# Two accumulator tiles in place of one, and a new timetable for the gated products after attention

## The chip, the cores and the metric

One core of a Trainium2 chip runs the whole program. Its engines each take their own instructions in order: TensorE (PE; its weight loads are shown as PEld), VectorE (DVE), ScalarE (ACT), GpSimd (POOL) and SyncE (SP), which issues nearly all DMAs. An engine whose next instruction has to wait for a semaphore holds everything behind it. The metric is the device time of one execution in microseconds.

## The reference, cut to what matters

```
q, k, v: (4, 8, 576, 64)             w_in: (512, 1024)  conv_w: (3, 1024)  w_out: (1024, 512)
q_rot, k_rot = rotate(q), rotate(k)                    # rotary tables
scores = q_rot @ k_rot^T / 8;  attn = softmax(scores)  # over 576 keys
x = (attn @ v), heads side by side                     # (4, 576, 512)
h = max(x @ w_in, 0)                                   # (4, 576, 1024)
conv_out = sum over k of conv_w[k] * h shifted by k-1  # three taps along the sequence
out = (h * sigmoid(conv_out)) @ w_out                  # (4, 576, 512)
```

The weights arrive as 64-bit floats and are turned into fp32 in the kernel.

## The kernel before, in words

**Pairs and steps.** Two heads of one batch make a pair: 16 pairs. The 576 queries of a pair are cut into four blocks of 128 and one of 64 for both heads, so a pair has five *steps*, s = 0 to 4, and the whole attention has 80, numbered n = 5p + s. A table `plan[n]` holds, for every step n, closures with a rank; they are run in the order of their ranks, and that order is the order of instructions on every engine (nothing is reordered afterwards).

**What a step holds.** PE makes the scores of step n (`emit_S`, L260, "S", tile `sp`); DVE takes two row maxima (L268, `negm`); ACT takes two exponentials (L272, `st`). PE turns the exponentials of step n-1 around (`emit_T`, L320, "the turn", tile `tp`) and ACT copies them into `pt` (L198). The last 64 keys of one head and the first of the other are turned by two small transposes (`emit_Trem`, L357, "the remainder's turn"), which write columns 320 to 383 of both accumulator banks and are copied to `pt` by DVE (L200). In the step after a pair's last one, n = 5p + 5, PE multiplies `pt` by v (`emit_E`, L388, two products of 20 matmuls, "E"); ACT copies each (L398, `xn`), DVE scales it some steps later (L402) by 1/sum, which reaches it by way of two DMAs (`rd`, `rb`), and ACT and POOL split it into a high and a low fp32r part (`xT`, L406, L407).

**The two products of the second stage.** From step 26 (`WIDE`) on the weights are ready, and steps also hold *units* of the first product (`emit_M1`, L421: 12 matmuls, 128 of the 1024 columns for 288 tokens) and *halves* of the second (`m2_half`, L519: 48 matmuls of 64 rows, 256 of the 512 output columns for 128 tokens). Behind a unit come, on other engines: ACT's max (L429, `rr`), three DVE taps ("the taps", L433 once, L435 twice, tile `c`), ACT's tanh (L441), DVE's gate (L444), ACT's high part (L452, `g`) and POOL's low part (L453). A half ends in an ACT copy (L533) of one bank, a DVE add (L534) of the other and a store. `UNITS` and `HALVES` say which step holds how many; `E` of step 5p + 5 ranks last.

**The timetable of what follows a unit.** `defer(k, fn)` puts a closure k *slots* ahead; a slot passes (`tick`) after each closure whose rank is in `onpe`, so after each piece of PE work. The taps, tanh, gate and split come 2, 5, 7 and 9 slots after the unit, wherever these slots fall.

**The accumulator.** `m_pair` takes, once a step, one tile `pm` of two banks (128 x 2 x 512 fp32) from a pool with one buffer, so the next step's tile is the same two banks. Units, halves, E and the remainder's turn of a step all live in it; `m_tile` hands out the two banks in turn.

**Other work of a pair.** Its q and k are loaded (L148 to L150, six DMAs each), rotated on POOL ("the rope", L189 six times, L192 three times) and turned on DVE (L233, L236, L242), 9 to 2 steps before the pair begins.

**The tail.** After the last step the pools are closed and the units and tiles that are left run back to back in six other banks (`mt`, L421 and L499): 16 units, and the tiles of the second product from the second half of tile 10 to tile 17.

Of the kernel before, what the change touches and what calls it, by code (L numbers as in the profile page):

```python
# [7 lines left out]
F32 = mybir.dt.float32  # L8
# [12 lines left out]
def attention_moe_kernel(ctx, tc, q, k, v, w_in, conv_w, w_out, tab, tabx, out):  # L21
# [49 lines left out]
    sinr = tabs[:, 576:640].rearrange("p (n i) -> p n i", n=2)  # L71
    ptctx = ExitStack()
    ptp = ptctx.enter_context(tc.tile_pool(name="ptp", bufs=1, side="right"))
    late = {"tail": False, "short": False, "u": 0}
    pt = ptp.tile([128, 9, S], F32, name="pt")

    slot = [0]
# [28 lines left out]

    def m_pair():
        if pair["n"] != late["n"]:
            pair.update(n=late["n"], ps=psum["m"].tile([128, 2, 512], F32, tag="m", name="pm"), k=0)
        return pair["ps"]  # L110

    def m_tile():
        if late["tail"]:
            return psum["t"].tile([128, 512], F32, tag="mt", name="mt")
        ps = m_pair()
        pair["k"] ^= 1
        return ps[:, 1 - pair["k"], :]

    raw = {}
    rot = {}  # L120
# [225 lines left out]
    def emit_Trem(p, s):  # L346
        x = ST[p, s].rearrange("p h k -> p (h k)")[:, 512:640]
        dst = pt[:, 8, 128 * s:128 * s + 128]
        if "m" not in psum:
            ps = spare(128)  # L350
            nc.tensor.transpose(ps, x, idf)
            after(lambda: evac("V", dst, ps))
            return
        ps = m_pair()[:, :, 320:384]
        for r in range(2):
            i = slice(64 * r, 64 * r + 64)
            nc.tensor.transpose(ps[:, r, :], x[i], idf[i, i])  # L357
        at(late["n"], 5, lambda: evac("V", dst.rearrange("p (r c) -> p r c", r=2), ps))

    rb = {}  # L360

# [46 lines left out]

        norms[p, j] = lambda: (norm(), defer(1, split))

    def emit_M1(blk, f):
        b, j = divmod(blk, 2)
        g, rr = late["g"], late["rr"]
        ps = m_tile()
        fs = slice(128 * f, 128 * f + 128)
        n = 3 * NK
        i = 0
        for kk in range(NK):
            xs = xslot[b, kk, j]
            for w, e in ((winh, 0), (winh, 1), (winl, 0)):  # L420
                nc.tensor.matmul(  # L421
                    out=ps[:, 0:XW], lhsT=w[:, kk, fs], rhs=xT[:, xs, e, :], start=(i == 0), stop=(i == n - 1)
                )
                i += 1
        if f == NF - 1:
            for kk in range(NK):
                free_slots.append(xslot.pop((b, kk, j)))
        r = rr[(blk * NF + f) % len(rr)]
        nc.scalar.activation(out=r[:, 1:XW], in_=ps[:, j:j + XW - 1], func=AF.Relu, scale=0.5)  # L429
        c = late["pc"].tile([128, HS], F32, tag="c", name="c")  # L430

        def conv():
            nc.vector.tensor_scalar(out=c, in0=r[:, j:j + HS], scalar1=cw[:, f:f + 1], scalar2=None, op0=ALU.mult)  # L433
            for e in (1, 2):
                nc.vector.scalar_tensor_tensor(  # L435
                    out=c, in0=r[:, j + e:j + e + HS], scalar=cw[:, 8 * e + f:8 * e + f + 1], in1=c,
                    op0=ALU.mult, op1=ALU.add,
                )

        def tanh():  # L440
            nc.scalar.activation(out=c, in_=c, func=AF.Tanh)  # L441

        def gate():
            nc.vector.scalar_tensor_tensor(  # L444
                out=c, in0=c, scalar=1.0, in1=r[:, j + 1:j + 1 + HS], op0=ALU.add, op1=ALU.mult
            )

        def split():
            o = 0
            for dst, n in g_pieces(blk, f):  # L450
                hi, lo = dst[:, 0, :], dst[:, 1, :]
                nc.scalar.activation(out=hi, in_=c[:, o:o + n], func=AF.Copy)  # L452
                nc.gpsimd.tensor_tensor(out=lo, in0=c[:, o:o + n], in1=hi.bitcast(F32), op=ALU.subtract)  # L453
                o += n
            ready.add((blk, f))

        lag = (1, 2, 3, 4) if late["short"] else (2, 5, 7, 9)
        for k, fn in zip(lag, (conv, tanh, gate, split)):
            defer(k, fn)

    LASTB = 2 * B - 1
    TAIL = (LASTB * HS + 127) // 128 * 128
# [24 lines left out]
    done_tt = set()  # L487

    def emit_M2(tt, part):
        cuts = 2 if tt in (len(HALVES) // 2, B * S // 128 - 1) else 1  # L490
        per, width = cuts * NF // 4, DM // cuts
        cut, part = divmod(part, 4 // cuts)
        cols = slice(width * cut, width * cut + width)
        if part == 0:
            ops[tt] = m_tile()
        for f in range(per * part, per * part + per):
            assert all((blk, f) in ready for blk in range(tt * 128 // HS, (tt * 128 + 127) // HS + 1))
            for i, (e, w) in enumerate(((0, wouth), (0, woutl), (1, wouth))):
                nc.tensor.matmul(  # L499
                    out=ops[tt][:, 0:width], lhsT=g_tile(tt, f, e), rhs=w[:, f, cols],  # L500
                    start=(f == 0 and i == 0), stop=(f == NF - 1 and i == 2),
                )
        if part == 4 // cuts - 1:
            done_tt.add(tt)
            ot = late["po"].tile([128, DM], F32, tag="ot", name="ot")[:, 0:width]
            nc.vector.tensor_copy(ot, ops.pop(tt)[:, 0:width])
            nc.sync.dma_start(out=out[tt * 128:tt * 128 + 128, cols], in_=ot)

    def m2_half(tt, cut):
        cols = slice(256 * cut, 256 * cut + 256)  # L510

        def run(fs):
            ps = m_pair()
            for f in fs:
                assert all((blk, f) in ready for blk in range(tt * 128 // HS, (tt * 128 + 127) // HS + 1))
                for i, (e, w) in enumerate(((0, wouth), (0, woutl), (1, wouth))):
                    for r in range(2):
                        rows = slice(64 * r, 64 * r + 64)
                        nc.tensor.matmul(  # L519
                            out=ps[:, r, 0:256], lhsT=g_tile(tt, f, e)[rows], rhs=w[rows, f, cols],  # L520
                            start=(f == 0 and i == 0), stop=(f == NF - 1 and i == 2),
                        )

# [3 lines left out]
        def second():  # L527
            run(range(NF // 2, NF))
            if cut:
                done_tt.add(tt)  # L530
            ps = m_pair()
            ot = late["po"].tile([128, 256], F32, tag="oh", name="oh", bufs=2)
            nc.scalar.activation(out=ot, in_=ps[:, 0, 0:256], func=AF.Copy)  # L533
            nc.vector.tensor_tensor(out=ot, in0=ot, in1=ps[:, 1, 0:256], op=ALU.add)  # L534
            nc.sync.dma_start(out=out[tt * 128:tt * 128 + 128, cols], in_=ot)

        return first, second
# [102 lines left out]
        wsteps += wcv[i][1:]  # L640

    WIDE = 26
    UNITS = dict([(n, 1) for n in (26, 27, 28, 29, 31, 32, 33, 34)])
    UNITS.update({36: 3, 38: 3, 41: 2, 44: 2, 47: 3, 49: 3, 53: 3, 56: 3, 58: 2, 64: 2, 67: 3, 69: 3, 73: 3, 76: 3, 78: 2})
    HALVES = [37, 39, 42, 43, 46, 48, 51, 52, 54, 57, 59, 61, 62, 63, 66, 68, 71, 72, 74, 77, 79]
    plan = {}
    onpe = (0, 0.5, 1, 2, 3, 4, 10)
    engines = {nc.tensor.engine, nc.vector.engine, nc.scalar.engine, nc.gpsimd.engine, nc.sync.engine}

    def at(n, rank, fn):  # L650
# [2 lines left out]
    def emit():  # L653
        with tc.manual_schedule(engines=engines):
# [17 lines left out]
            for p in range(1, NP):  # L672
                n = STEPS * p
                for i, part in enumerate("qk"):
                    if p > 1:
                        at(n - 9 + 2 * i, 19, lambda p=p, part=part: load(p, part))
                    at(max(n - 6 + i, 0) if p > 1 else 0, 18, lambda p=p, part=part: rope(p, part))
                    at(max(n - 4 + 2 * i, 2), 0.45, lambda p=p, part=part: emit_TQ(p, part))
                at(n + 3, 19, lambda p=p: load_v(p))
            for p in range(NP):  # L680
                n = STEPS * p
# [29 lines left out]
            at(12, 3, conv_cw)  # L711
            at(14, 2, turn_cw)
            for n, k in UNITS.items():
                for _ in range(k):
                    blk, f = divmod(late["u"], NF)
                    late["u"] += 1
                    at(n, 2, lambda blk=blk, f=f: emit_M1(blk, f))
            for i, n in enumerate(HALVES):
                for k, u in enumerate(m2_half(i // 2, i % 2)):
                    at(n, 2 + k, u)  # L720
            for n in range(max(plan) + 1):
                late["n"] = n
                late["short"] = n >= STEPS * NP - 3
                if n == WIDE:
                    wctx.close()
                    ectx.close()
                    psum_pools(actx, s=2, t=2, m=1)
                    gpool = ctx.enter_context(tc.tile_pool(name="gpool", bufs=1))
                    late["pc"] = ctx.enter_context(tc.tile_pool(name="pc", bufs=4))
                    late["po"] = ctx.enter_context(tc.tile_pool(name="po", bufs=1))  # L730
# [5 lines left out]
                while plan.get(n):  # L736
                    e = min(plan[n], key=lambda e: e[:2])
                    plan[n].remove(e)
                    e[2]()
                    if e[0] in onpe:  # L740
                        tick()
            while due:
                tick()
# [8 lines left out]
            first = [lambda f=f: emit_M1(last, f) for f in range(NF)]  # L752
            second = [lambda f=f: emit_M1(LASTB, f) for f in range(NF)]
            t = HS * last // 128
            prev = m2_units(len(HALVES) // 2, t)[len(HALVES) % 2 * 2:]
            seq = prev[:len(prev) - NF]
            for a, b in zip(first, prev[len(prev) - NF:]):
                seq += [a, b]
            for u in seq + second + m2_units(t, B * S // 128):
# [54 lines left out]
```

## Time and profile before

| | |
|---|---|
| time, median of 3 runs | 555.95 us (555.48 to 556.79) |
| the profiled execution's own time | 555.18 us |
| its span, first to last instruction | 553.4 us, mean granted TensorE clock 0.988 |
| PE busy | 466.4 us (84%), 4692 instructions |
| PEld busy | 363.6 us (66%) |
| DVE busy | 355.9 us (64%), 689 |
| ACT busy | 314.8 us (57%), 842 |
| POOL busy | 297.1 us (54%), 479 |
| chain that ended last | PE 44%, DVE 24%, ACT 21%, issue 4%, DMA 3% |

Busy time is the union of an engine's instructions over the whole span; the chain is followed back from the last instruction, each time to what released it. Both are averages over four stages that differ: attention with the conversion of the weights (to 128.3 us), steps 26 to 35, steps 36 to 79, and the tail from 482.1 us. The steps can be found in the trace by their scores: each run of eight L260 matmuls opens one.

### The profile page before, as it was taken

The numbers are of one execution on the slowest core, as the hardware profiler recorded it, in microseconds if no ns is written. First come the engines' busy times: TensorE is split into PE (matmuls) and PEld (weight loads), VectorE is DVE, ScalarE is ACT, GpSimd is POOL, SyncE is SP. The second block draws the span as 40 slices with busy tenths as digits, with TensorE's granted clock in tenths as the row PEclk, the third lists the DMA queues.
The fourth block names the chain that finished last, engine by engine and source line by source line (L and its number), as shares of the span: only waits on it lengthen the run. The fifth ranks groups of instructions, "written<-read, shape, count | busy, mean of one in ns | idle before, by whom it ended". The sixth has DMA issues, their size and how long they took to land.

```text
span 553.4 us, 12460 instructions
## 1 busy us (share of the span) xinstructions
PE 466.4 (84%) x4692; PEld 363.6 (66%) x4692; DVE 355.9 (64%) x689; ACT 314.8 (57%) x842; POOL 297.1 (54%) x479
## 2 busy tenths in 40 slices
PE   2877777868899878898888978998879887899997
PEld 1344545535676766767667776786758766699986
DVE  4798889983878565645675666446765626256941
ACT  2678777874866556646565555656548536334510
POOL 3799979998478373372475236445293013123430
PEclk9999999988999999999999998999999998999999
DMA  9787675553332331233306023252222001001011
GB/s 213 161 164 178 160 187 144 125 108 77 55 81 51 65 74 32 55 75 75 75 23 127 34 48 70 62 108 51 45 55 63 12 23 33 32 9 39 2 38 58
DMA packets 140849, 42.73 MB, mean 77 GB/s; under 512 B 132189, under 2 KB 135797, under 8 KB 140789
## 3 DMA queue, kind: packets, MB, share of 16 engines
q1 hardware_dynamic: 139444, 41.54, 33.7%
q8 instruction: 37, 0.61, 0.4%
q10 hardware_dynamic: 1344, 0.39, 0.3%
q14 instruction: 24, 0.19, 0.1%
HBM read 37.12 MB, written 4.79 MB: 76 GB/s over the span
## 4 chain that ended last, share of the span: by engine, by line
PE 44%; DVE 24%; ACT 21%; issue 4%; DMA 3%; POOL 2%; SPq 1%; ACTq 0%; DVEq 0%; POOLq 0%
PE pm L421 9%; ACT st L272 8%; DVE negm L268 8%; PE pm L388 8%; PE mt L499 8%; PE sp L260 6%; ACT pt L198 6%; PE pm L519 5%; PE mt L421 5%; DVE c L435 4%; ACT rr L429 3%; PE tp L320 1%; DVE c L444 1%; DVE c L433 1%; DVE wt L557 1%
## 5 line engine op out<-in xcount | busy, mean ns | idle before, releaser
L268 DVE TENSOR_REDUCE negm<-sp 128x1 f32<-128x576 f32 x144 | 102.2, 746 | 42.0 <-PE sp L260 35.7
L453 POOL TENSOR_TENSOR g<-c,g 128x288 fp32r<-128x288 f32 (+4 forms) x88 | 53.5, 623 | 133.3 <-ACT g L452 133.1
L272 ACT ACTIVATE st<-sp,negm 128x576 f32<-128x576 f32 x128 | 93.8, 739 | 53.8 <-DVE negm L268 53.3
L421 PE MATMUL pm<-xT,winh 128*128 128x290 f32 x384 | 85.9, 316 | 25.7 <-ACT rr L429 25.7
L260 PE MATMUL sp<-kT,qT 64*128 64x288 f32 (+4 forms) x556 | 97.9, 460 | 3.8 <-DVE kT L236 2.6
L198 ACT ACTIVATE pt<-tp 128x512 f32<-128x512 f32 (+3 forms) x176 | 84.0, 529 | 6.5 <-PE tp L320 6.1
L421 PEld LDWEIGHTS pm<-xT,winh 128*128 128x128 f32 x384 | 62.4, 194 | 33.1 <-ACT rr L429 31.6
L435 DVE SCALAR_TENSOR_TENSOR c<-rr,cw,c 128x288 f32<-128x288 f32 x128 | 77.0, 602 | 4.5
L407 POOL TENSOR_TENSOR xT<-xn,xT 128x290 fp32r<-128x290 f32 x32 | 27.4, 869 | 75.5 <-ACT xT L406 75.5
L320 PEld LDWEIGHTS tp<-idf,st 64*128 64x128 f32 x1024 | 43.1, 139 | 33.2 <-ACT st L272 22.7
L519 PE MATMUL pm<-wouth,g 64*128 64x256 f32 x672 | 64.3, 281 | 0.0
L320 PE MATMUL tp<-idf,st 64*128 64x64 f32 x1024 | 50.5, 228 | 16.1 <-ACT st L272 15.6
L260 PEld LDWEIGHTS sp<-kT,qT 64*128 64x128 f32 (+1 forms) x556 | 47.4, 177 | 23.8 <-issue 9.9
L189 POOL TENSOR_TENSOR rk<-rk,tabt 128x192 f32<-128x192 f32 x90 | 57.1, 669 | 10.8 <-DVE c L435 7.3
L388 PE MATMUL pm<-pt,vm 128*64 128x290 f32 x368 | 50.0, 413 | 13.3 <-ACT xn L398 8.2
L189 POOL TENSOR_TENSOR rq<-rq,tabt 128x192 f32<-128x192 f32 x90 | 56.4, 661 | 6.9 <-DMA rq<-q 6.6
L421 PE MATMUL pm<-xT,winl 128*128 128x290 f32 x192 | 57.8, 301 | 0.0
L519 PEld LDWEIGHTS pm<-wouth,g 64*128 64x128 f32 x672 | 56.2, 186 | 0.0
L519 PE MATMUL pm<-woutl,g 64*128 64x256 f32 x336 | 50.4, 276 | 0.0
L429 ACT ACTIVATE rr<-pm 128x289 f32<-128x289 f32 x48 | 20.1, 419 | 49.3 <-PE pm L421 49.3
L200 DVE COPY pt<-pm 128x128 f32<-128x128 f32 x44 | 12.6, 287 | 54.3 <-ACT rr L429 54.2
L388 PEld LDWEIGHTS pm<-pt,vm 128*64 128x64 f32 x368 | 25.4, 136 | 33.2 <-ACT xn L398 13.9
(108 smaller groups left out, 865.0 us busy)
## 6 DMA issues: line engine op xcount, KB each, us to landing
rq<-q SPq DMA_DIRECT2D x30, 144.0 KB
rq<-q SPq DMA_DIRECT2D x60, 72.0 KB
rk<-k SPq DMA_DIRECT2D x30, 144.0 KB
rk<-k SPq DMA_DIRECT2D x60, 72.0 KB
w<-moe_w_in SPq DMA_DIRECT2D x8, 512.0 KB
vm<-v SPq DMA_DIRECT2D x32, 128.0 KB
w<-moe_w_out SPq DMA_DIRECT2D x8, 512.0 KB
out<-oh SPq DMA_DIRECT2D x21, 128.0 KB
```

Of the source, the lines that this page charges most:

```text
L189: nc.gpsimd.tensor_tensor(out=y, in0=y, in1=tabt[:, a:a + 3], op=ALU.mult)
L198: nc.scalar.activation(out=out, in_=in_, func=AF.Copy, scale=1.0 if sc is None else sc)
L260: nc.tensor.matmul(out=out, lhsT=qt[64 * h:64 * h + 64, c], rhs=kt[64 * h:64 * h + 64, a:a + n], start=True, stop=True)
L268: reds.setdefault((p, s), []).append(lambda: nc.vector.tensor_reduce(out=nm, in_=sc, axis=AX.XY if len(sc.shape) == 3 else AX.X, op=ALU.ma ...
L272: lambda: nc.scalar.activation(out=dst, in_=sc, func=AF.Exp, bias=nm, scale=1.0, accum_out=sm)
L320: nc.tensor.transpose(ps[r][:, 64 * k:64 * k + 64], x[i], idf[i, i])
L388: nc.tensor.matmul(out=xp[64 * h:64 * h + 64, :], lhsT=vmain[p][:, h, i, :] if i < 4 else vrem[:, h, :], rhs=pt[:, 2 * i + h if i < 4 else ...
L421: nc.tensor.matmul(out=ps[:, 0:XW], lhsT=w[:, kk, fs], rhs=xT[:, xs, e, :], start=(i == 0), stop=(i == n - 1))
L435: nc.vector.scalar_tensor_tensor(out=c, in0=r[:, j + e:j + e + HS], scalar=cw[:, 8 * e + f:8 * e + f + 1], in1=c, op0=ALU.mult, op1=ALU.add,)
L453: nc.gpsimd.tensor_tensor(out=lo, in0=c[:, o:o + n], in1=hi.bitcast(F32), op=ALU.subtract)
L499: nc.tensor.matmul(out=ops[tt][:, 0:width], lhsT=g_tile(tt, f, e), rhs=w[:, f, cols], start=(f == 0 and i == 0), stop=(f == NF - 1 and i = ...
L519: nc.tensor.matmul(out=ps[:, r, 0:256], lhsT=g_tile(tt, f, e)[rows], rhs=w[rows, f, cols], start=(f == 0 and i == 0), stop=(f == NF - 1 an ...
```

## The change

The two accumulator banks become two tiles of one bank each, from a pool with two buffers, so that each bank has its own waits. The remainder's turn and its copy are made for each bank apart (two copies of 128 x 64 instead of one of 128 x 128). `UNITS` gives two units each to the steps with s = 1 and s = 3 and `HALVES` one half each to those with s = 2 and s = 4 (some of the last ones lie a step off; s = 0 keeps the two E products of the pair before); from step 36 on there are 36 units and 18 halves where there were 40 and 21. The four units and three halves that are left over go to the tail. The taps, tanh, gate and split of a unit are tied to steps (this one or the next, and so on) and to ranks within them. From step 26 on a slot passes after the maxima and no longer after the scores. For pairs from the eighth on, q and k are loaded together ten steps ahead, rotated eight and seven steps ahead and turned five steps ahead.

```diff
     def m_pair():
         if pair["n"] != late["n"]:
-            pair.update(n=late["n"], ps=psum["m"].tile([128, 2, 512], F32, tag="m", name="pm"), k=0)
+            pair.update(n=late["n"], ps=[psum["m"].tile([128, 512], F32, tag="m", name="pm") for _ in range(2)], k=0)
         return pair["ps"]
...
-        ps = m_pair()[:, :, 320:384]
         for r in range(2):
             i = slice(64 * r, 64 * r + 64)
-            nc.tensor.transpose(ps[:, r, :], x[i], idf[i, i])
-        at(late["n"], 5, lambda: evac("V", dst.rearrange("p (r c) -> p r c", r=2), ps))
+            ps = m_pair()[r][:, 320:384]
+            nc.tensor.transpose(ps, x[i], idf[i, i])
+            at(late["n"], 5, lambda dst=dst[:, i], ps=ps: evac("V", dst, ps))
...
-        lag = (1, 2, 3, 4) if late["short"] else (2, 5, 7, 9)
-        for k, fn in zip(lag, (conv, tanh, gate, split)):
-            defer(k, fn)
+        if late["tail"]:
+            for k, fn in enumerate((conv, tanh, gate, split)):
+                defer(k + 1, fn)
+        else:
+            n = late["n"] + last
+            for k, rank, fn in ((0, 0.3 if last else 2.5, conv), (1, 0.1, tanh), (2 - last, 0.3, gate), (3 - last, 0.1, split)):
+                at(n + k, rank, fn)
...
-    UNITS.update({36: 3, 38: 3, 41: 2, 44: 2, 47: 3, 49: 3, 53: 3, 56: 3, 58: 2, 64: 2, 67: 3, 69: 3, 73: 3, 76: 3, 78: 2})
-    HALVES = [37, 39, 42, 43, 46, 48, 51, 52, 54, 57, 59, 61, 62, 63, 66, 68, 71, 72, 74, 77, 79]
+    UNITS.update({n: 2 for n in (36, 38, 41, 43, 46, 48, 51, 53, 56, 58, 61, 63, 66, 69, 71, 74, 77, 79)})
+    HALVES = [37, 39, 42, 44, 47, 49, 52, 54, 57, 59, 62, 64, 67, 68, 72, 73, 76, 78]
...
-                        at(n - 9 + 2 * i, 19, lambda p=p, part=part: load(p, part))
-                    at(max(n - 6 + i, 0) if p > 1 else 0, 18, lambda p=p, part=part: rope(p, part))
-                    at(max(n - 4 + 2 * i, 2), 0.45, lambda p=p, part=part: emit_TQ(p, part))
+                        at(n - 10 if n - 10 >= WIDE - 1 else n - 9 + 2 * i, 19, lambda p=p, part=part: load(p, part))
+                    early = n - 10 >= WIDE - 1
+                    at(n - 8 + i if early else max(n - 6 + i, 0) if p > 1 else 0, 18, lambda p=p, part=part: rope(p, part))
+                    at(n - 5 if early else max(n - 4 + 2 * i, 2), 0.45, lambda p=p, part=part: emit_TQ(p, part))
...
-                    psum_pools(actx, s=2, t=2, m=1)
+                    psum_pools(actx, s=2, t=2, m=2)
...
-                    if e[0] in onpe:
+                    if e[0] in onpe and e[0] != (0 if n >= WIDE else 0.2):
                         tick()
...
-            prev = m2_units(len(HALVES) // 2, t)[len(HALVES) % 2 * 2:]
-            seq = prev[:len(prev) - NF]
+            prev = m2_units(len(HALVES) // 2, t)
+            seq = [lambda f=f: emit_M1(last - 1, f) for f in range(late["u"] % NF, NF)] + prev[:len(prev) - NF]
```

What this does to the instructions is seen best on two engines. On PE, a step with units in pair 8 (steps 41 to 44) stood so before: the remainder's turn (L357), a unit of 12 matmuls (L421) and the first matmuls of the next unit, with the engines whose semaphores an instruction waits for.

```order
L357 MATMUL pm<-idf,st 128x64 [waits DVE_49,Activation_49]
L357 MATMUL pm<-idf,st 128x64
L421 MATMUL pm<-xT,winh 128x290 x2
L421 MATMUL pm<-xT,winl 128x290
L421 MATMUL pm<-xT,winh 128x290 x2
L421 MATMUL pm<-xT,winl 128x290
L421 MATMUL pm<-xT,winh 128x290
L421 MATMUL pm<-xT,winh 128x290 [waits Pool_49]
L421 MATMUL pm<-xT,winl 128x290
L421 MATMUL pm<-xT,winh 128x290
L421 MATMUL pm<-xT,winh 128x290 [waits Pool_49]
L421 MATMUL pm<-xT,winl 128x290
L421 MATMUL pm<-xT,winh 128x290 [waits Activation_49]
```

A step with units of the same stretch stands so now:

```order
L357 MATMUL pm<-idf,st 128x64 [waits DVE_49,Activation_49]
L357 MATMUL pm<-idf,st 128x64 [waits DVE_49]
L421 MATMUL pm<-xT,winh 128x290 x2
L421 MATMUL pm<-xT,winl 128x290
L421 MATMUL pm<-xT,winh 128x290 x2
L421 MATMUL pm<-xT,winl 128x290
L421 MATMUL pm<-xT,winh 128x290 x2
L421 MATMUL pm<-xT,winl 128x290
L421 MATMUL pm<-xT,winh 128x290 x2
L421 MATMUL pm<-xT,winl 128x290
L421 MATMUL pm<-xT,winh 128x290 x2
L421 MATMUL pm<-xT,winl 128x290
```

The second unit's first matmul no longer waits for ACT; instead each of the two remainder's turns has a wait of its own.

On DVE, the pieces behind the three units of step 53 stood so before (`rr0` to `rr3` are the units' max outputs, `c` their taps, `sp` the scores):

```order
L444 SCALAR_TENSOR_TENSOR c_3491<-c_3491,rr0_1702 128x288
L433 TENSOR_SCALAR c_3663<-rr1_1703,cw_80 128x288
L435 SCALAR_TENSOR_TENSOR c_3663<-rr1_1703,cw_80,c_3663 128x288 x2
L200 COPY pt_94<-pm_3644 128x128
L433 TENSOR_SCALAR c_3681<-rr2_1704,cw_80 128x288
L435 SCALAR_TENSOR_TENSOR c_3681<-rr2_1704,cw_80,c_3681 128x288 x2
L268 TENSOR_REDUCE negm_3709<-sp_3712 128x1
L268 TENSOR_REDUCE negm_3709<-sp_3713 128x1
L433 TENSOR_SCALAR c_3695<-rr3_1705,cw_80 128x288
L435 SCALAR_TENSOR_TENSOR c_3695<-rr3_1705,cw_80,c_3695 128x288 x2
```

And so now, behind the two units of step 53 (s = 3), with the maxima of step 54 among them:

```order
L444 SCALAR_TENSOR_TENSOR c_3373<-c_3373,rr0_1716 128x288
L444 SCALAR_TENSOR_TENSOR c_3387<-c_3387,rr1_1717 128x288
L433 TENSOR_SCALAR c_3552<-rr2_1718,cw_80 128x288
L435 SCALAR_TENSOR_TENSOR c_3552<-rr2_1718,cw_80,c_3552 128x288 x2
L200 COPY pt_94<-pm_3531 128x64
L200 COPY pt_94<-pm_3532 128x64
L268 TENSOR_REDUCE negm_3232<-sp_3586 128x1
L433 TENSOR_SCALAR c_3566<-rr3_1719,cw_80 128x288
L435 SCALAR_TENSOR_TENSOR c_3566<-rr3_1719,cw_80,c_3566 128x288 x2
L538 TENSOR_TENSOR oh_3677<-oh_3677,pm_3623 128x256
L200 COPY pt_94<-pm_3622 128x64
L200 COPY pt_94<-pm_3623 128x64
```

The first unit's taps still stand ahead of the step's remainder copies; the last unit's taps now stand behind the next step's maxima, and the gates come right behind the maxima of the step with the next units.

## Rows read from the trace of the kernel before

**Rows 1.** Windows, stage by stage: length, busy us per engine, PEclk, DMA share, GB/s

```profile
...
128.30:179.60 51.30, 46.23 (x444) 34.23 (x442) 38.02 (x73) 34.34 (x89) 35.37 (x63) 1.00 0.35 71
179.60:473.80 294.20, 254.24 (x2888) 209.53 (x2888) 173.61 (x361) 166.51 (x445) 129.88 (x208) 0.99 0.26 57
...
482.10:553.40 71.30, 68.15 (x410) 61.34 (x408) 38.02 (x75) 20.86 (x67) 19.36 (x34) 1.00 0.08 29
...
```

**Rows 2.** Waits of PE in steps 36 to 79: us in total, times, longest

```profile
...
PE pm L421 <- ACT rr L429: 25.7, 25, 2.2
PE pm L388 <- ACT xn L398: 6.4, 8, 1.5
PE pm L357 <- DVE pt L200: 2.9, 3, 1.0
...
```

**Rows 3.** Chain that ended last, steps 53 to 56: start us, us, what

```profile
...
301.22 1.89 PE pm L421 x12
303.11 1.12 PE sp L260 x8
...
304.93 2.88 PE pm L519 x47
307.81 0.95 PE sp L260 x8
308.76 0.33 PE tp L320 x9
...
309.50 2.69 PE pm L388 x20
...
312.67 2.66 PE pm L388 x20
...
```

**Rows 4.** Timeline of step 56: start us, us, instruction, [idle before <-releaser]

```profile
...
315.27 1.24 PE L260 MATMUL sp<-kT,qT 64*128 64x288 f32 x8
...
316.54 1.42 DVE L268 TENSOR_REDUCE negm<-sp 128x1 f32<-128x576 f32 x2 [4.22 <-PE sp L260]
...
316.98 3.35 POOL L189 TENSOR_TENSOR rk<-rk,tabt 128x192 f32<-128x192 f32 x6
316.99 0.53 PE L421 MATMUL pm<-xT,winh 128*128 128x290 f32 x2
317.33 0.74 ACT L272 ACTIVATE st<-sp,negm 128x576 f32<-128x576 f32 x1 [1.18 <-DVE negm L268]
...
318.78 1.08 ACT L198 ACTIVATE pt<-tp 128x512 f32<-128x512 f32 x2
...
319.73 0.43 ACT L429 ACTIVATE rr<-pm 128x289 f32<-128x289 f32 x1
320.19 0.37 DVE L433 TENSOR_SCALAR c<-rr,cw 128x288 f32<-128x288 f32 x1 [1.55 <-ACT rr L429]
320.21 0.54 PE L421 MATMUL pm<-xT,winh 128*128 128x290 f32 x2 [1.35 <-ACT rr L429]
...
320.60 1.51 DVE L435 SCALAR_TENSOR_TENSOR c<-rr,cw,c 128x288 f32<-128x288 f32 x2
...
324.96 0.29 DVE L200 COPY pt<-pm 128x128 f32<-128x128 f32 x1 [2.85 <-ACT rr L429]
...
325.56 0.52 DVE L435 SCALAR_TENSOR_TENSOR c<-rr,cw,c 128x288 f32<-128x288 f32 x1
...
```

**Rows 5.** Waits of PE from 120 to 180 us

```profile
...
PE pm L388 <- DVE pt L200: 2.0, 2, 1.7
...
PE pm L388 <- ACT xn L398: 1.3, 2, 0.7
...
```

**Rows 6.** Chain that ended last, start of the tail

```profile
...
482.12 2.94 PE mt L499 x24
485.06 1.61 PE mt L421 x12
486.67 1.40 PE mt L499 x6
...
```

More of the change, by code (lines that the diff above doesn't have):

```diff
@@ L73, in attention_moe_kernel @@
     ptp = ptctx.enter_context(tc.tile_pool(name="ptp", bufs=1, side="right"))
-    late = {"tail": False, "short": False, "u": 0}
+    late = {"tail": False, "u": 0}
     pt = ptp.tile([128, 9, S], F32, name="pt")
@@ L116, in m_tile @@
         pair["k"] ^= 1
-        return ps[:, 1 - pair["k"], :]
+        return ps[1 - pair["k"]]
     raw = {}
@@ L409, in emit_E, with emit_M1 @@
         norms[p, j] = lambda: (norm(), defer(1, split))
-    def emit_M1(blk, f):
+    def emit_M1(blk, f, last=False):
         b, j = divmod(blk, 2)
@@ L489, in emit_M2 @@
     def emit_M2(tt, part):
-        cuts = 2 if tt in (len(HALVES) // 2, B * S // 128 - 1) else 1
+        cuts = 2 if tt == B * S // 128 - 1 else 1
         per, width = cuts * NF // 4, DM // cuts
@@ L519, in run @@
                         nc.tensor.matmul(
-                            out=ps[:, r, 0:256], lhsT=g_tile(tt, f, e)[rows], rhs=w[rows, f, cols],
+                            out=ps[r][:, 0:256], lhsT=g_tile(tt, f, e)[rows], rhs=w[rows, f, cols],
                             start=(f == 0 and i == 0), stop=(f == NF - 1 and i == 2),
@@ L532, in second @@
             ot = late["po"].tile([128, 256], F32, tag="oh", name="oh", bufs=2)
-            nc.scalar.activation(out=ot, in_=ps[:, 0, 0:256], func=AF.Copy)
-            nc.vector.tensor_tensor(out=ot, in0=ot, in1=ps[:, 1, 0:256], op=ALU.add)
+            nc.scalar.activation(out=ot, in_=ps[0][:, 0:256], func=AF.Copy)
+            nc.vector.tensor_tensor(out=ot, in0=ot, in1=ps[1][:, 0:256], op=ALU.add)
             nc.sync.dma_start(out=out[tt * 128:tt * 128 + 128, cols], in_=ot)
@@ L642, in attention_moe_kernel @@
     WIDE = 26
-    UNITS = dict([(n, 1) for n in (26, 27, 28, 29, 31, 32, 33, 34)])
-    UNITS.update({36: 3, 38: 3, 41: 2, 44: 2, 47: 3, 49: 3, 53: 3, 56: 3, 58: 2, 64: 2, 67: 3, 69: 3, 73: 3, 76: 3, 78: 2})
-    HALVES = [37, 39, 42, 43, 46, 48, 51, 52, 54, 57, 59, 61, 62, 63, 66, 68, 71, 72, 74, 77, 79]
+    UNITS = {n: 1 for n in (26, 27, 28, 29, 31, 32, 33, 34)}
+    UNITS.update({n: 2 for n in (36, 38, 41, 43, 46, 48, 51, 53, 56, 58, 61, 63, 66, 69, 71, 74, 77, 79)})
+    HALVES = [37, 39, 42, 44, 47, 49, 52, 54, 57, 59, 62, 64, 67, 68, 72, 73, 76, 78]
     plan = {}
-    onpe = (0, 0.5, 1, 2, 3, 4, 10)
+    onpe = (0, 0.2, 0.5, 1, 2, 3, 4, 10)
     engines = {nc.tensor.engine, nc.vector.engine, nc.scalar.engine, nc.gpsimd.engine, nc.sync.engine}
@@ L713, in emit @@
             for n, k in UNITS.items():
-                for _ in range(k):
+                for i in range(k):
                     blk, f = divmod(late["u"], NF)
                     late["u"] += 1
-                    at(n, 2, lambda blk=blk, f=f: emit_M1(blk, f))
+                    at(n, 2, lambda blk=blk, f=f, last=i == k - 1: emit_M1(blk, f, last))
             for i, n in enumerate(HALVES):
@@ L720, in emit @@
                     at(n, 2 + k, u)
-            for n in range(max(plan) + 1):
+            n = -1
+            while any(plan.values()):
+                n += 1
                 late["n"] = n
-                late["short"] = n >= STEPS * NP - 3
                 if n == WIDE:
```

## The prediction

> **What bounds the kernel now.** I read the windows by stage first, since the work differs between them. PE is busy for 254.2 of the 294.2 us of steps 36 to 79, for 46.2 of 51.3 us in steps 26 to 35, and for 68.2 of 71.3 us in the tail; DVE and ACT are busy for less than 60% of steps 36 to 79 [rows 1]. So PE sets the pace from step 26 on, and what can be won is its idle time, 40 us in steps 36 to 79. Who ends that idle time stands in the table of waits: 25.7 us are 25 waits of a unit for the copy (`rr`) of the unit before it, 6.4 us are 8 waits of a pair's second E product for the copy of the first, and 2.9 us are three waits of the remainder's turn for DVE's copy of the last one [rows 2]. The instructions ahead of step 26 do not change, and the tail has next to no idle time [rows 1].
>
> The timeline of step 56 shows what the first kind of wait is. The first unit starts at 316.99 and needs 1.9 us; the second one starts only at 320.21, right after ACT's copy of the first, although it writes the other bank [rows 4]. That copy began at 319.73, since on ACT it stands behind both exponentials (from 317.33) and both copies of the turn (from 318.78) [rows 4]. One tile for two banks makes a unit wait for ACT's whole step.
>
> **The change part by part.** *Two tiles.* The second unit writes a tile nobody has read in this step, and in the order of the new program its first matmul waits for nothing on ACT; the second E product likewise. A third unit in a step would come back to the first tile, but now there are two at most. Removed: 25.7 + 6.4 us of waits [rows 2]. To see what is late next I price each kind of step from the chain, with PE never waiting for an accumulator:
> - between the products lie scores and turns: 303.11 to 304.93, 1.82 us, behind a unit, and 315.27 to 316.99, 1.72 us, in front of one [rows 3, 4];
> - a step with two units: 1.72 + 2 x 1.89 = 5.50 us; with a half: 1.82 + 2.88 = 4.70 us [rows 3, 4];
> - a step with E: 0.95 + 0.33 + 0.41 + 2.69 + 2.66 = 7.04 us, with the 0.41 us wait before E kept and the wait between the two products (312.19 to 312.67) gone [rows 3].
>
> Steps 36 to 79 now hold 18 x 5.50 + 18 x 4.70 + 8 x 7.04 = 99.0 + 84.6 + 56.3 = 239.9 us. The same prices applied to before (40 units in 15 steps, 21 halves, 8 E steps with 0.48 us more each) give 15 x 1.72 + 40 x 1.89 + 21 x 4.70 + 8 x 7.52 = 260.3 us, and with the 25.7 + 2.9 us of the other waits 288.9, against 294.2 measured: the prices are 2% short, no more, and part of that is waits of other kinds.
>
> *Does DVE or ACT become the next bound?* I follow one stretch with the delays of step 56: scores begin at 0, maxima at 1.27, exponentials at 2.06, copies of the turn at 3.51, `rr` of the first unit at 4.46, its taps at 4.92 [rows 4]. The taps take 0.41 + 2 x 0.52 = 1.45 us with POOL away and 0.41 + 1.51 = 1.92 us under a rope [rows 4], and behind them stand the two copies of the remainder: they are done at 6.7 or 7.2 us. PE wants to write the remainder into these tiles at 5.50 + 1.8 = 7.3. So it just fits. In the step with a half, DVE has maxima 1.4, taps 1.45, the E scalings, add and copies, and ends some 1.1 us behind the half; the next remainder's turn comes 1.7 us behind it. That fits too. In the step with E DVE and ACT have 7 us and no taps. I therefore take 0.5 us a pair for waits that stay, 4.4 us over 8.8 pairs; the ends are 0 and 2.5 us (both steps with units 1.25 us late). Result: 244 us, ends 236.6 (without the 0.41 us waits too) and 262.
>
> *The remainder's copies.* One DVE copy of 128 x 128 takes 0.29 us [rows 4]; for two of 128 x 64 the trace has no row. Between nothing and 0.29 us more per step, 36 steps of the stage; I take 0.1, hidden in DVE's 120 us of idle time [rows 1], and counted above in the fit.
>
> *The units and halves that go to the tail.* There a unit takes 1.61, a quarter tile 1.40 and a half tile 2.94 us [rows 6]. Added: four units 6.44, tile 9 whole 5.60, tile 10 whole in place of its second half 2.66: 14.7 us, with PE as full as it is there now [rows 1]; DVE and ACT, busy for 38.0 and 20.9 of 71.3 us there, can follow.
>
> *Steps 26 to 35* have one unit each as before. The waits of the second E product, 1.3 us, go [rows 5]. So does the longest wait of E for DVE's remainder copy, 1.7 us in step 26 [rows 5], because that copy no longer waits for `rr` of the other bank, as it did in step 56 for 2.85 us [rows 4]. 3.0 us won, ends 0 and 5 (all idle time of the stage, [rows 1]). In step 80 the second E product's wait goes as well, 0.5 us.
>
> *Loads, ropes and turns of q and k* move earlier for nine pairs, at no cost while POOL, busy for 130 of 294 us [rows 1], hides them: a pair's two ropes take twice 3.35 us for their larger part (L189) [rows 4], and less for L192, of a pair's 27. In SP's queue twelve loads now stand together behind the `rb` transfers of the pair before and ahead of the next v and output transfers, and are needed two steps later. If that cover is gone, POOL's low parts wait behind a rope, then a tap for its `c` buffer (rival 3).
>
> *The timetable* has no price of its own: the same instructions, whose waiting is in the stretch above.
>
> **Sum.** 553.4 - 3.0 - (294.2 - 244.3) - 0.5 + 14.7 = 514.7 us of span. The profiled execution took 555.18 us, 1.8 more than its span, and the median of the runs is 0.8 above that: 517 us.
>
> **The rivals.** *1. The taps hold up the remainder.* The stretch above has about 0.1 us to spare under a rope. The ropes of a pair move from beside s = 4 and 0 to beside s = 2 to 4, where the taps and gates run. By the trace a tap beside a rope takes 0.75 instead of 0.52 us [rows 4]; four of them, and two gates at the same 0.23 us more, make DVE 1.4 us later a pair, and such a delay passes on through maxima, exponentials and `rr`. At 1.3 us a pair more the time is 517 + 8.8 x 1.3 = 528. For it: the small slack; against it: the last rope stands in step 68, and the E step has time to catch up. The Trainium skill (SBUF — State Buffer, Who interferes with whom) has a harsher rule: a VectorE instruction with two SBUF inputs and a GpSimd one that reads SBUF exclude each other for a whole instruction. By the rule each of these six would wait up to a piece of the rope, 0.56 us (3.35 / 6), in the seven pairs with ropes: 24 us, a time of 541. The trace does not agree with the whole of it: it shows 0.23 us per tap.
>
> *2. Waits only move.* If a unit's wait for ACT comes back as a wait of the remainder's turn in every step behind units, 18 waits of 1.3 us, about as long as those of the second unit, would leave 517 - 4 + 23 = 536. Against it: the remainder comes 1.8 us later in its step than the second unit did.
>
> *3. Slower than before.* Ropes that wait for their loads hold up POOL's low parts, these hold up the four `c` buffers, a tap waits for a buffer on DVE and the maxima behind it stop PE. It decides from 517 + 39 on: 4.5 us a pair. By the stretch the low parts of the units of s = 1 are done 6 us before the buffer is wanted again, so loads would have to come about 10 us late in every pair. Nothing in the waits of PE speaks for it.
>
> *4. No change:* the second unit still waits. Then only the moved work counts: 14.7 against 4 x 1.89 + 3 x 2.88 = 16.2 us, 554. The order of the new program speaks against it.
>
> **Chances.** Forecast, 503 to 523: 0.64. Rivals 1 and 2, 523 to 540: 0.28. Rival 3: 0.04; rival 4: 0.02; better than 503: 0.02. The range follows from the ends of the terms: 553.4 - 5 - 57.6 - 1 + 14.7 + 2.6 = 507, less another 1% of the stage for the prices, 504; and 553.4 - 0 - 32 + 14.7 + 2.6 = 538.7, which takes in most of rivals 1 and 2. Faster by over 0.2%, about what a measurement of this kernel can tell from no change: 0.94; within: 0.02; slower: 0.04.
>
> **What would show it.** In the new profile: no wait of a unit for `rr` and none of the second E product for `xn`; steps of 5.5, 4.7 and 7.0 us; steps 36 to 79 in about 244 us with PE busy for 95% of it; a tail of 86 us. Wrong would be: waits of the remainder's turn for DVE's copies of more than 10 us in all (rivals 1 and 2); DVE waiting for POOL at the taps (rival 3); a tail longer than 86 us.

## The result, and the profile after

The changed kernel takes 512.25 us (median of 4 runs, 510.98 to 513.61), the kernel before, on the same chip, 556.37 us (4 runs): a ratio of 0.920, 95% interval 0.9157 to 0.9244. Faster, by 44 us; 517.0 with a range of 504 to 539 was forecast. The profiled execution took 510.98 us, 1.9 more than its span of 509.1.

The windows by stage of the changed kernel answer to [rows 1]: steps 26 to 35, steps 36 to 79, step 80, tail. The columns are length, busy us of PE, PEld, DVE, ACT and POOL, granted clock, DMA share, GB/s.

```profile
128.60:179.90 51.30, 46.77 (x436) 34.66 (x432) 38.64 (x79) 33.77 (x88) 34.14 (x62) 1.00 0.36 71
179.90:417.00 237.10, 229.27 (x2699) 193.40 (x2699) 172.89 (x375) 162.48 (x427) 130.48 (x202) 1.00 0.35 69
417.00:423.00 6.00, 5.80 (x53) 3.96 (x53) 3.73 (x10) 2.84 (x9) 1.77 (x2) 1.00 0.03 6
423.00:509.10 86.10, 82.84 (x480) 73.78 (x478) 47.63 (x93) 26.25 (x82) 24.78 (x40) 1.00 0.09 32
```

Nearly all of the gain is in steps 36 to 79: 237.1 us instead of 294.2, with PE busy for 97% of them instead of 86%; step 80 adds 2.3 us. The tail is 14.8 us longer, as it has more work. The first row begins 0.8 us late: the scores of step 26 begin at 127.78, so steps 26 to 35 take 52.1 us, 0.8 more than before. Who ends PE's idle time in steps 36 to 79 (waits of PE: us in total, times, longest) answers to [rows 2]:

```profile
PE pm L357 <- DVE pt L200: 6.5, 9, 1.8
PE sp L260 <- ACT st L272: 1.3, 1, 1.3
```

The 25 waits of a unit for `rr` and the eight of the second E product for `xn` are gone. What is left is the remainder's turn waiting for DVE. The chain that ended last in steps 54 to 57 shows where that comes from (start us, us, what):

```profile
278.53 0.74 DVE c L433
...
279.29 0.74 DVE c L435
...
280.05 0.73 DVE c L435
280.79 0.28 DVE pt L200 x2
...
281.07 0.31 PE pm L357 x2
281.38 2.82 PE pm L523 x46
284.20 0.97 PE sp L260 x8
285.17 0.30 PE tp L320 x10
285.48 5.03 PE pm L388 x40
...
295.44 0.38 DVE c L433
...
295.85 0.53 DVE c L435
...
296.40 0.52 DVE c L435
```

Before step 54's half the chain runs over DVE: the three taps of the unit ahead (2.2 us beside a rope), then the remainder's copies, and only then the remainder's turn and the half. In step 57, with POOL off the ropes, the same three taps take 1.4 us. The E step has no pause any more: both products are one piece of 5.03 us [rows 3 shows 2.69 and 2.66 with a wait between them].

Steps 36 to 40, the first pair with units in twos, take 30.7 us, the five pairs behind them 26.7 each. The chain that ended last at the end of step 35 and in step 36 shows the late start:

```profile
181.69 1.12 POOL rk L192 x2
...
182.83 0.78 DVE kT L236
...
184.84 0.65 DVE negm L268
...
185.52 1.55 ACT st L272 x4
187.07 0.97 ACT pt L198 x2
188.05 0.31 ACT rr L429
...
190.34 0.27 DVE pt L200 x2
```

POOL's rope of pair 9's k ends late, DVE has stood for 3.1 us before the turn of that k (pairs are counted from 1), and everything of step 36 queues up behind it: maxima, exponentials, the turn's copies, `rr`, and at last the remainder's copies, for which the remainder's turn ahead of step 37's half waits 1.8 us, the longest wait above. PE's 1.3 us before scores are of the same origin.

### The profile page after: what moved, and what is told of

Its sections match the earlier page's. It is cut to its first block, busy times and chain, and to the rows that moved or that the text cites. A ratio compares the mean times of both kernels' runs of the same rounds, so it can differ in the third digit from the quotient of the medians.

```text
span 509.1 us, 12329 instructions
## 1 busy us (share of the span) xinstructions
PE 463.4 (91%) x4572; PEld 365.8 (72%) x4572; DVE 368.3 (72%) x731; ACT 316.4 (62%) x839; POOL 301.6 (59%) x479
## 4 chain that ended last, share of the span: by engine, by line
PE 46%; DVE 21%; ACT 16%; POOL 8%; DMA 5%; issue 3%; SPq 2%; DVEq 0%; ACTq 0%; POOLq 0%
PE mt L503 10%; PE pm L388 9%; ACT st L272 8%; PE pm L523 7%; PE sp L260 6%; PE mt L421 6%; DVE negm L268 6%; ACT pt L198 5%; DVE c L435 4%; PE pm L421 3%; POOL rk L189 2%; DMA rq<-q 2%; PE tp L320 2%; POOL rq L189 2%; DVE c L433 2%
## 5 line engine op out<-in xcount | busy, mean ns | idle before, releaser
L260 PE MATMUL sp<-kT,qT 64*128 64x288 f32 (+4 forms) x556 | 103.1, 472 | 4.8 <-DVE kT L236 2.8
L435 DVE SCALAR_TENSOR_TENSOR c<-rr,cw,c 128x288 f32<-128x288 f32 x128 | 78.6, 614 | 4.5
L421 PE MATMUL pm<-xT,winh 128*128 128x290 f32 x352 | 74.5, 305 | 0.0
L260 PEld LDWEIGHTS sp<-kT,qT 64*128 64x128 f32 (+1 forms) x556 | 49.2, 179 | 24.4 <-issue 13.2
L189 POOL TENSOR_TENSOR rq<-rq,tabt 128x192 f32<-128x192 f32 x90 | 57.6, 675 | 13.7 <-DMA rq<-q 13.7
L189 POOL TENSOR_TENSOR rk<-rk,tabt 128x192 f32<-128x192 f32 x90 | 58.7, 685 | 7.8 <-DMA rk<-k 7.8
L421 PEld LDWEIGHTS pm<-xT,winh 128*128 128x128 f32 x352 | 56.2, 189 | 1.8
L523 PE MATMUL pm<-wouth,g 64*128 64x256 f32 x576 | 56.5, 281 | 0.0
L433 DVE TENSOR_SCALAR c<-rr,cw 128x288 f32<-128x288 f32 x64 | 29.4, 460 | 34.1 <-ACT rr L429 34.1
L523 PEld LDWEIGHTS pm<-wouth,g 64*128 64x128 f32 x576 | 52.6, 186 | 0.0
L421 PE MATMUL pm<-xT,winl 128*128 128x290 f32 x176 | 52.0, 296 | 0.0
L444 DVE SCALAR_TENSOR_TENSOR c<-c,rr 128x288 f32<-128x288 f32 x64 | 38.0, 615 | 9.4 <-ACT c L441 9.4
L441 ACT ACTIVATE c<-c 128x288 f32<-128x288 f32 x64 | 28.3, 442 | 24.7 <-DVE c L435 24.5
```

Source lines behind the costliest of these rows:

```text
L189: nc.gpsimd.tensor_tensor(out=y, in0=y, in1=tabt[:, a:a + 3], op=ALU.mult)
L260: nc.tensor.matmul(out=out, lhsT=qt[64 * h:64 * h + 64, c], rhs=kt[64 * h:64 * h + 64, a:a + n], start=True, stop=True)
L421: nc.tensor.matmul(out=ps[:, 0:XW], lhsT=w[:, kk, fs], rhs=xT[:, xs, e, :], start=(i == 0), stop=(i == n - 1))
L435: nc.vector.scalar_tensor_tensor(out=c, in0=r[:, j + e:j + e + HS], scalar=cw[:, 8 * e + f:8 * e + f + 1], in1=c, op0=ALU.mult, op1=ALU.add,)
L523: nc.tensor.matmul(out=ps[r][:, 0:256], lhsT=g_tile(tt, f, e)[rows], rhs=w[rows, f, cols], start=(f == 0 and i == 0), stop=(f == NF - 1 an ...
```

## The experiments

Times are medians; ratios are to the kernel before, measured beside it on the same chip. Each edit is shown against the changed kernel unless it says otherwise.

**One two-bank tile again**, all else changed.

```
-            pair.update(n=late["n"], ps=[psum["m"].tile([128, 512], F32, tag="m", name="pm") for _ in range(2)], k=0)
+            pair.update(n=late["n"], ps=psum["m"].tile([128, 2, 512], F32, tag="m", name="pm"), k=0)
```

> The changed kernel with the two banks back in one tile (one buffer); units, halves, timetable and loads stay as changed. Theory (the loss was one tile's shared waits): the second unit of each of 18 steps waits again for ACT's copy of the first, which ends 4.9 us into the step while the first unit ends at 3.6, so 18 x 1.3 = 23 us, and the second E product 8 x 0.5 = 4 us: 512 + 27 = 539 us, 533 to 546, with waits of L421 for rr back at 18 times some 1.3 us. Rival (the new order of units and of what follows them brought the gain): 511 to 518 us.

Measured: 540.84 us, ratio 0.9686 (0.9652 to 0.9719). Its waits of PE from step 26 on:

```profile
PE pm L421 <- ACT rr L429: 24.7, 18, 4.1
PE pm L388 <- ACT xn L398: 5.6, 11, 0.5
```

Eighteen waits, one for each step with two units. The timetable does not take them away; the tiles do.

**Only the two tiles**, in the kernel before: the hunks of the diff at L109, L117, L351 to L358, L520, L533 and L727, nothing else.

> The kernel before with the two banks as two tiles and nothing else. Theory: the waits of the second unit (25.7 us) and of the second E product (6.4 us) go; a third unit comes back to the first tile, but ACT's copy of it ends 4.9 us into the step and the second unit at 5.5, so it waits for nothing; some of the gain comes back as waits of the remainder's turn, since DVE's copies still stand among three units' taps: 524 to 533 us. Rival (order brought the gain): over 545 us.

Measured: 516.72 us, ratio 0.9265 (0.923 to 0.930), 41 us from this alone, more than expected. A third unit, which comes back to the first tile, hardly waits: 0.6 us in one wait. Its waits of PE in steps 36 to 79:

```profile
PE pm L357 <- DVE pt L200: 4.2, 5, 0.9
PE pm L388 <- ACT pt L198: 3.1, 4, 1.0
PE pm L357 <- ACT g L452: 0.9, 1, 0.9
PE pm L421 <- ACT rr L429: 0.6, 1, 0.6
...
```

**Units, halves and tail of before**, all else changed.

```
-    UNITS.update({n: 2 for n in (36, 38, 41, 43, ...
+    UNITS.update({36: 3, 38: 3, 41: 2, 44: 2, 47: 3, ...
-    HALVES = [37, 39, 42, 44, 47, 49, ...
+    HALVES = [37, 39, 42, 43, 46, 48, ...
```

> The changed kernel with the units and halves of before (up to three units in a step, 40 units and 21 halves from step 36 on, the tail of before); two tiles, the timetable of taps, tanh, gates and splits and the early loads stay. Theory: PE's work is the same to 2 us wherever it stands (16.2 us in the stage against 14.7 in the tail), so only waits differ: three units' taps in a row keep DVE 1.5 us later in 10 steps, 512 + 2 + 10 x 0.5 to 1.5 = 519 to 529 us. Rival (units in twos brought most): over 535 us.

Measured: 539.42 us, ratio 0.9674 (0.9645 to 0.9703): far off. Next to the run before it there are three more differences (the order of the steps, the early loads, the early ropes and turns), and something among them costs 23 us. Timeline of POOL and of DVE around the longest wait of PE (8.6 us, the remainder's turn at 211.72):

```profile
203.31 3.32 POOL L189 TENSOR_TENSOR rk<-rk,tabt 128x192 f32<-128x192 f32 x6
206.59 1.67 POOL L192 TENSOR_TENSOR rk<-rk 128x192 f32<-128x192 f32 x3
208.22 2.35 POOL L453 TENSOR_TENSOR g<-c,g 128x288 fp32r<-128x288 f32 x3
...
209.04 0.88 DVE L433 TENSOR_SCALAR c<-rr,cw 128x288 f32<-128x288 f32 x1 [7.45 <-POOL g L453]
```

Three low parts stand behind two ropes on POOL; a tap has no `c` buffer until the first of them is done, and DVE stands for 7.45 us. That is rival 3 of the prediction, in another kernel: three units in a step and the early ropes.

**The same with the loads, ropes and turns of before** (of the change only the tiles and the order of the steps are left).

```
-  at(n - 10 if n - 10 >= WIDE - 1 else n - 9 + 2 * i, 19, ... load
-  at(n - 8 + i if early else max(n - 6 + i, 0) if p > 1 else 0, 18, ... rope
-  at(n - 5 if early else max(n - 4 + 2 * i, 2), 0.45, ... emit_TQ
+  at(n - 9 + 2 * i, 19, ... load
+  at(max(n - 6 + i, 0) if p > 1 else 0, 18, ... rope
+  at(max(n - 4 + 2 * i, 2), 0.45, ... emit_TQ
```

> The two tiles with the units, halves and tail of before and the loads, ropes and turns of before: only the order of the steps (scores, turn, products, taps) is the new one. With the new loads as well this took 539.4 us, and its trace has two stops (8.6 us of PE before the remainder's turn, 6.1 us before an E product) during which DVE waits 7.45 and 6.58 us at the taps L433 for POOL's low parts L453, which stand behind a rope. Theory (three units in a step fill the four c buffers, and ropes that come one or two steps earlier hold the low parts that free them): without the early ropes the stops go, and the time is 512 to 520, about that of the two tiles alone (516.7). Rival (the new order of the steps does not suit three units in a step): the stops stay, 530 to 540.

Measured: 511.88 us, ratio 0.9195 (0.9178 to 0.9212). The two long stops are gone. So the early loads, ropes and turns together cost 27 us beside three units in a step (the ropes are what the trace shows in the longest stops; they were not tried alone here), and the order of the steps by itself gains a little (511.9 against 516.7; the intervals of the ratios do not overlap).

**The changed kernel with the loads, ropes and turns of before** (the same edit).

> The changed kernel with loads, ropes and turns of q and k at the steps of before. Theory: they are hidden either way, and the early ones cost a little: SP's queue stood before the v loads (1.4 us in step 30), DVE stood 3.1 us for a rope in step 35 (some 3 us on PE in steps 36 and 37), and the ropes beside s = 3 make the remainder's turn wait 0.6 us in 7 pairs; against this the turn of k comes back to s = 3 ahead of taps. 504 to 511 us. Rival (the early loads are needed, since DVE and POOL are full): over 515 us.

Measured: 501.08 us, ratio 0.8981 (0.8959 to 0.9003), below the 504 to 511 expected and the fastest of all: 57 us below before on the same chip, 11 below the changed kernel. Its steps 36 to 79 (columns as above) and its chain in steps 59 to 61:

```profile
179.90:408.00 228.10, 226.11 (x2697) 191.06 (x2696) 167.36 (x374) 162.31 (x427) 124.85 (x201) 1.00 0.34 72
```

```profile
300.82 2.88 PE pm L523 x48
303.70 0.97 PE sp L260 x8
304.67 0.30 PE tp L320 x10
304.97 5.04 PE pm L388 x40
310.00 1.17 PE sp L260 x8
311.18 0.49 PE tp L320 x16
311.67 0.06 PE pm L357 x2
311.73 3.45 PE pm L421 x24
315.18 1.17 PE sp L260 x8
```

PE is busy for 99% of the stage, and in these steps the chain never leaves PE. The early loads were to cost nothing; they cost 11 us. The next four runs look for the part of them that does.

**Early from pair 9 on** (counted from 1; the changed kernel begins with pair 8).

```
-  early = n - 10 >= WIDE - 1
+  early = n - 10 >= WIDE
```

(The load's condition likewise.)

> The changed kernel, but the early loads, ropes and turns begin with pair 9 instead of pair 8; pair 8 is loaded, turned and transposed where it was before. The changed kernel loses 8.7 us of span against the one with all of the old loads: 4.2 us of it in steps 36 to 40 (30.4 against 26.2 us) and about 0.8 us in each of the next five pairs. Theory (the 4.2 us are the start: pair 8's loads are issued while pair 7's k is not yet turned, and the ropes wait for them): without it 507 to 508 us, steps 36 to 40 in 26.3 us, and a pair afterwards still 26.5. Rival (any pair that begins the early loads pays): the 4 us only move to steps 41 to 45, 510 to 512.

Measured: 510.71 us, ratio 0.9167 (0.9128 to 0.9206).

**Early loads, late ropes.**

```
-  at(n - 8 + i if early else ..., 18, ... rope
-  at(n - 5 if early else ..., 0.45, ... emit_TQ
+  at(n - 6 + i if early else ..., 18, ... rope
+  at(n - 4 if early else ..., 0.45, ... emit_TQ
```

> The changed kernel with only the loads early: ropes stand where they stood before (beside s = 4 and 0), and both turns one step before the pair. Theory (the 0.8 us a pair are the ropes beside s = 2 to 4, whose taps take 0.73 to 0.88 us instead of 0.52 and hold up the remainder's copies): 501 to 504 us, a pair of 25.8 us, the waits of the remainder's turn for DVE down from 7.6 to about 3.5 us. Rival (the early loads themselves hold SP's queue, so that v and the outputs come late): 507 to 511, with waits for vm or for output tiles.

Measured: 502.41 us, ratio 0.9024 (0.9007 to 0.9041).

**Early loads and ropes, turns one step later** (the second line of the edit above alone).

> The changed kernel with the early loads and ropes, but both turns of q and k one step later, one step before their pair as in the run with late ropes (502.4 us). Theory (the ropes' place beside s = 2 to 4 is what costs, by slower taps and gates on DVE): steps with s = 3 stay at 5.2 us instead of 4.4, a pair at 26.5 us, the time 508 to 513. Rival (the turns, 1.8 us of DVE in the step where the pair before has its first units, are what costs): 501 to 504.

Measured: 506.45 us, ratio 0.9076 (0.9045 to 0.9106), between the two. (The slow half that the expectation puts at s = 3 is the one at s = 4, counted as in the sections above.)

**A second buffer for the raw k** (`bufs=2` for the tile `rk`).

> The changed kernel with a second buffer for the raw k, so that a pair's k is loaded without waiting for the turn of the pair before, and v behind it on SP's queue neither. Theory (the start of the early loads costs 4 to 5 us because k's load waits until that turn, and the rope behind it, the turn of k and the scores are late in turn): steps 26 to 40 in 78 us instead of 81.7, no wait for vm, the time 507 to 509. Rival (the start is late because POOL has three ropes to do there beside its low parts): 511 to 513, with DVE's turn of k still waiting 2 to 3 us for POOL.

Measured: 510.46 us, ratio 0.9155 (0.9116 to 0.9194).

What these say together, in us worked out from the first matmul of the scores (L260) of steps 26, 36, 41, 66 and 76 in each trace:

| kernel | span | steps 26–35 | 36–40 | a pair of 41–65 | 66–75 |
|---|---|---|---|---|---|
| changed | 509.1 | 52.1 | 30.7 | 26.7 | 52.5 |
| early from pair 9 | 509.8 | 56.5 | 26.7 | 26.7 | 52.2 |
| second raw k | 509.7 | 51.7 | 30.8 | 26.7 | 52.4 |
| turns later | 504.8 | 51.5 | 27.3 | 26.7 | 52.2 |
| early loads, late ropes | 500.7 | 50.9 | 27.4 | 25.8 | 52.0 |
| loads, ropes and turns as before | 500.4 | 51.4 | 26.3 | 25.9 | 52.1 |

Each row is one trace, so a few tenths say nothing. The column of steps 26 to 35 says little below 2 us: the granted clock of this stage was 1.00 in the changed kernel and 0.97 in the three runs at the foot of the table.

The ropes' place is 0.8 us a pair: all four kernels with early ropes have pairs of 26.7 us, both others 25.8 or 25.9. The loads alone, with both turns one step before the pair, cost little: 0.3 us of span in these traces, 1.3 us by the medians.

The rest is lost once, 4 to 5 us, but not to one cause. In the changed kernel it is lost in steps 35 to 37, to the turn of pair 9's k. POOL's rope of pair 9's q had waited 6.40 us for its load, which SP issued at 163.03, right behind the `rb` transfers of the pair before (the last at 162.33); the rope of k came behind it, and the turn waited for that:

```profile
169.86 3.86 POOL L189 TENSOR_TENSOR rq<-rq,tabt 128x192 f32<-128x192 f32 x6 [6.40 <-DMA rq<-q]
...
177.30 3.85 POOL L189 TENSOR_TENSOR rk<-rk,tabt 128x192 f32<-128x192 f32 x6
...
182.83 0.78 DVE L236 STREAM_TRANSPOSE kT<-rk 128x576 f32<-128x576 f32 x1 [3.11 <-POOL rk L192]
```

With the turns one step later that turn waits for nothing, and steps 36 to 40 are 3.4 us shorter. In the run from pair 9 on the same turn waits 2.54 us, but step 35 is long there (11.2 us, against 6.6 with the old loads) for another reason. PE waits for v, whose loads stand in SP's queue behind those of k. Then its E products take 7.3 us instead of 5.0, at granted clocks of 0.83 (from 176 to 180 us) and 0.75 (180 to 184), mixtures of the 2.4 and 1.2 GHz levels:

```profile
177.60 3.61 PE L388 MATMUL pm<-pt,vm 128*64 128x290 f32 x15 [2.43 <-DMA vm<-v]
```

So my theory of a start that pair 8 pays fell: steps 36 to 40 take 26.7 us there, but the time stayed. Its rival, that any pair that begins pays those 4 us, is not shown either: pair 8 begins in the changed kernel, whose steps 26 to 35 are 0.8 us longer than with the old loads, or some 2 us by an estimate that counts the clock (0.03 of 51 us). The two losses are of like size, and their causes differ. The expectation of the run with later turns had the ropes and the turns as rivals; both cost, in different stretches.

The second raw k tells only part of it. The wait for v went, but DVE's turn of k still waited 2.0 us for POOL (3.1 in the changed kernel), and steps 36 to 40 are not shorter. In that run the clock fell too: after 188 to 190 us with PE nearly idle, 190 to 194 was granted 0.60 (a mixture of the 2.4 and 1.2 GHz levels), and the half there ran slowly:

```profile
188.00:190.00 2.00, 0.23 (x7) 0.12 (x3) 1.93 (x6) 0.55 (x3) 0.97 (x1) 0.94 0.53 153
190.00:194.00 4.00, 4.00 (x44) 4.00 (x46) 3.38 (x7) 2.79 (x7) 0.00 (x0) 0.60 1.17 185
```

So k's load is not what makes POOL late: with two buffers it waits for no turn, and in both traces POOL goes from the rope of q over the low parts of `xT` to that of k without a pause. Both share the wait of q's rope for its load (4.09 us here, 6.40 in the changed kernel) and the work behind it. Whether q's load or the closeness of the two ropes weighs more was not tried; a turn one step later avoids most of the cost either way.

## Why the prediction was right, and where its terms were not

**The mechanism is shown.** The waits for `rr` and `xn`, 32.1 us, came from one tile for two banks: with one tile they are back, and two tiles alone make 41 of the 44 us. Units in twos and the moved halves bring another 11 us (511.9 to 501.1, both with the old loads), the order of the steps 4 to 5, and the early loads, ropes and turns take 11 back. The edits are not independent: these three cost 27 us with three units in a step and 11 with two.

**Steps 36 to 79: 244.3 forecast, 237.1 measured.** The halves with their waits came out right in sum: 18 x 4.70 + 4.4 = 89.0 was forecast, and the 18 steps with halves measure 90.6, though unevenly, 4.5 us at s = 2 and 5.3 at s = 4, where the taps ahead run beside a rope, and 7.1 in step 37 with the late start. The other two prices were too high. An E step takes 6.5 instead of 7.04 us (4.3 us in the eight): the 0.41 us wait before E that I kept is gone as well, and the products take 5.03 instead of 5.35. A step with two units takes 5.0 to 5.3 instead of 5.50 us, step 36 apart: 1.72 us of scores and turns were right, but two units back to back take 3.45 us (the chain of the run with the old loads), not twice 1.89. That price held a start of its own: a unit's first two matmuls take 0.53 or 0.54 us [rows 4], two in mid-stream 0.43. What the rest of the 0.33 us is, no row shows.

**Steps 26 to 35: −3.0 forecast, +0.8 measured.** This term had a wrong reason. I had the 1.7 us wait of E in step 26 go, since the remainder's copy would no longer wait for `rr` of the other bank. But it stayed. By the timeline the copies in step 26 came right after the `rr` of the unit that shares a tile with one of the two remainders; why one read should stand behind another there the trace does not tell:

```profile
132.25 0.43 ACT L429 ACTIVATE rr<-pm 128x289 f32<-128x289 f32 x1
132.71 0.36 DVE L200 COPY pt<-pm 128x64 f32<-128x64 f32 x2 [1.55 <-ACT rr L429]
```

The second E product's waits did go, but the v loads now stand in SP's queue behind the early k loads, which stand until DVE has turned the k of the pair before. The timeline has k's loads at last at 145.30, one us after that turn began, v's behind them, and PE waiting for v (tile `vm`):

```profile
144.34 0.77 DVE L236 STREAM_TRANSPOSE kT<-rk 128x576 f32<-128x576 f32 x1
145.30 0.31 SPq L148 DMA_DIRECT2D rk<-k  x1
...
148.42 0.44 SPq L160 DMA_DIRECT2D vm<-v  x1
...
151.24 0.67 PE L388 MATMUL pm<-pt,vm 128*64 128x290 f32 x2 [1.42 <-DMA vm<-v]
```

I named that queue and its order, and then gave it no price; pair 9's q stood in it too, as shown above.

**"At no cost while POOL … hides them" failed.** POOL had the time, as I counted it (130.5 of 237 us busy). For this term I looked for the cover on the wrong engine; rival 1 had the right one. A rope beside a tap is paid on DVE, and after the tiles are split DVE is what PE waits for: 0.8 us a pair, by the run with late ropes. And a turn that is put where its rope is not sure to be done makes DVE wait in its queue, with the maxima behind it: 3.4 us once, by the run with the turns a step later. That the time came so near the forecast is partly luck. These 9 to 11 us (span and median) were met by prices that were too high by about as much: had the early loads, ropes and turns been free, as I said, the time would have been 501.1 us, below the range of 504 to 539.

**Tail and step 80.** The tail takes about 86 us, as forecast. Step 80 takes 6.0 instead of 8.3 us ([rows 1], between the stages), 2.3 less rather than 0.5; both E products are one piece of 5.1 us there too.

**The rivals.** Rival 1 happened, smaller than its price: 0.8 us a pair in place of 1.3, and only where ropes run, and the lower prices elsewhere covered it. The rule of the Trainium skill that I set against it (SBUF — State Buffer, Who interferes with whom: a VectorE instruction with two SBUF inputs and a GpSimd one that reads SBUF lock each other out for a whole instruction) is not borne out to its full size in the new trace either: the tap L435, which has two such inputs, loses 0.21 us beside a rope whose instructions take 0.55 us or more. Rival 2 did not happen: nine waits of the remainder's turn, 6.5 us together, in place of eighteen at 1.3 us. Rival 3 did not happen in the changed kernel, where no tap waits for POOL (its first link did: a rope that waits for its load), but the run with the old units and the early loads and ropes shows that it was near. Rival 4 is excluded by the waits.

## What to carry to other kernels

When an engine waits for the reader of a bank that it does not write, look whether two banks share one tile: splitting it was worth more here than the whole rearranged timetable. Work on an engine with half its time free is still not free when it slows an engine on the critical path; price it by the instructions that run beside it. And an instruction put into an in-order queue earlier than its input is sure to be there costs its wait times everything queued behind it: the best version found is the change without its early loads, ropes and turns, 501.1 us.

## What the hardware showed

Taps and ropes slow each other: the tap L435 takes 0.52 us alone and 0.74 beside a rope. L433, which reads one tensor and a column of scalars, takes 0.38 us alone and 0.74 beside the rope in the chain of the changed kernel, but not always as much: 0.46 at 199.58 us in the run with the old units. The rope's six instructions (L189) take 3.32 us while DVE stands, in the fence of the run with the old units, and 4.11 us in the same run beside taps and gates:

```profile
196.40 4.11 POOL L189 TENSOR_TENSOR rq<-rq,tabt 128x192 f32<-128x192 f32 x6
```
